# One shared set of PSUM banks for wide and narrow results, and ten loads issued by a second engine, in a scheduled attention and mixer kernel

## Chip, cores and metric

The kernel runs on one core of one Trainium2 chip. The metric is the device time of one execution in microseconds (us), less is better. A profiled execution also has a span, the time from its first to its last instruction, which is about 1.8 us shorter. Profiles are single executions: that of the kernel before took 214.4 us, 1.8 us less than its median, so a difference of two spans can be off by some us, and the medians decide. "Before" and "after" are the kernel without and with the change.

## The reference

Two parts run one after the other. The first is a recurrence over 768 steps for 4 batches and 8 heads of 40 numbers, from six inputs of 3.9 MB each. The second mixes its output over the tokens and the channels.

```python
for t in range(S):                                     # S = 768
    y[:, :, t] = einsum('bhd,bhde->bhe', rt, state)
    Sa = einsum('bhde,bhe->bhd', state, at)
    state = state * wt[:, :, None, :] - einsum('bhd,bhe->bhde', Sa, bt) + einsum('bhd,bhe->bhde', vt, kt)
# ... x = y with the heads side by side
theta = x @ w_theta
yr = einsum('ts,bsd->btd', w_tok_r, x * cos(theta))
yi = einsum('ts,bsd->btd', w_tok_i, x * sin(theta))
u = x + yr + yi
out = u + maximum(u @ w_ch, 0)
```

The kernel cuts the recurrence into 24 tiles of 128 tokens (6 in each batch). For each tile it loads w, a, k, b and v (r comes for two tiles at a time), makes decay products, transposes, four 128x1024 score products ("lamu", "lamv", "psi", "phi") with a masked eviction (a copy out of PSUM) each, and small products for the state. The mixer's rows ("row") need all of a batch, and the work of later tiles is laid over them.

## The kernel before

The kernel is written as a list of 1,457 operations. Each has an engine, an estimated cost, and the keys that it reads and writes. A list scheduler in the kernel lays the operations out in time by priority, assigns the banks of PSUM (the memory that takes TensorE's results, used here as eight banks), and emits the instructions in the order of the estimated starts. Nothing is reordered on the chip: in the traces each engine takes its instructions in this order, all 3,344 matmuls among them. The scheduler thus gives a planned length (208.2 us before). A framework beneath the kernel adds the semaphores.

```python
BANKS, DOUBLE = 8, 4
SP_DEPTH = 3600.0
# ...
def find(o):                                   # the scheduler looks for a free bank, or a pair
    n = o.new[1]
    if n == 2:
        c = [(max(bank_free[b], bank_free[b + 1]), (b, b + 1))
             for b in range(0, DOUBLE, 2)
             if not bank_held[b] and not bank_held[b + 1]]
        return min(c) if c else None
    c = [(bank_free[b], (b,)) for b in range(DOUBLE, BANKS) if not bank_held[b]]
    return min(c) if len(c) > o.spare else None
# ...
doubles = [psum.tile([128, 2, 512], FP32, name=f"ps_d{i}") for i in range(DOUBLE // 2)]
singles = [psum.tile([128, 512], FP32, name=f"ps_s{i}") for i in range(BANKS - DOUBLE)]
def ps(key):
    h = plan.home[key]
    return doubles[h[0] // 2] if len(h) == 2 else singles[h[0] - DOUBLE]
# ...
def loads(i):                                  # w, k, b, a, v of tile i, all from SyncE
    for key, dst, src in load(i):
        add("SP", "load", i, lambda dst=dst, src=src: nc.sync.dma_start(out=dst, in_=src),
            650, [], [key], work=1030)
# ...
for o in plan.order():                         # emission
    # ... (ScalarE's table loads)
    o.fn()
```

So four of the eight banks are two pairs, each one tile of two banks, for the scores. The other four are four tiles of one bank each, for transposes, rows and small products.

## Time and profile before

| | before |
|---|---|
| time, median (lowest to highest) | 216.2 us (215.5 to 216.7) |
| span of the profiled run | 212.6 us |
| length that the kernel's own scheduler planned | 208.2 us |
| TensorE: 3,344 matmuls, streaming need | 169.6 us |
| TensorE beyond streaming: changes of row mode / gaps over 60 ns / small ones | 20.1 / 11.4 / 3.8 us |
| changes between 64-row and 128-row matmuls | 130 |

The two TensorE lines need a word. The profile's busy time counts a matmul from start to end, but matmuls overlap. The Trainium skill, "Perfetto Trace Analysis", section "Identifying the Most-Contended Engine", says for this reason that matmul busy time is not a good measure of closeness to the limit, and this trace agrees: 195.1 us busy against 169.6 us of streaming. I therefore add the times from one matmul's start to the next one's. The least time in which one follows another of its kind is streaming (56 ns for 128 columns, 136 for 320). What goes beyond it at a change of row mode, in a gap over 60 ns, or in small steps, is the second line.

From the page of the kernel before: the span, TensorE's busy time, and the engines' shares of the chain that ended last.

```profile
span 212.6 us, 8107 instructions
...
PE 195.1 (92%) x3344; PEld 156.3 (74%) x3344; DVE 165.5 (78%) x252; ACT 148.6 (70%) x340; POOL 117.4 (55%) x173
...
PE 78%; DVE 7%; ACT 4%; issue 4%; DMA 3%; POOL 2%; SPq 1%; DVEq 0%; ACTq 0%; POOLq 0%
```

From the table of windows of the kernel before: for each stretch its length, then each engine's busy time with its instruction count, the granted TensorE clock, the DMA share and GB/s.

```profile
0.00:10.00 10.00, 3.84 (x39) 2.90 (x39) 6.33 (x48) 3.82 (x7) 3.39 (x14) 1.00 0.92 168
...
40.00:50.00 10.00, 8.94 (x194) 7.43 (x194) 8.53 (x9) 9.39 (x21) 8.43 (x13) 1.00 0.93 172
...
60.00:100.00 40.00, 38.72 (x716) 31.61 (x714) 33.40 (x43) 33.32 (x74) 30.71 (x45) 1.00 0.93 165
100.00:150.00 50.00, 49.93 (x911) 41.11 (x908) 43.85 (x56) 38.64 (x90) 30.43 (x43) 1.00 0.92 176
```

TensorE is short of work in the first 60 us (12.8 us idle, 6.2 of them in the first 10), where the DMA engines are full; after that it is hardly idle.

The rows of the mixer, in the groups of instructions by line, show how little TensorE waits (last field: its idle time just before these instructions):

```profile
L724 PE MATMUL ps_s<-zr,wtok_r 128*128 128x320 bf16 x144 | 40.7, 300 | 0.0
L724 PE MATMUL ps_s<-zi,wtok_i 128*128 128x320 bf16 x144 | 40.6, 299 | 0.0
```

And from the timeline (start, duration, instruction), a piece of one row, whose matmuls start every 130 to 140 ns:

```profile
151.11 0.30 PE L724 MATMUL ps_s<-zr,wtok_r 128*128 128x320 bf16 x1
...
151.24 0.30 PE L724 MATMUL ps_s<-zi,wtok_i 128*128 128x320 bf16 x1
...
151.38 0.30 PE L724 MATMUL ps_s<-zr,wtok_r 128*128 128x320 bf16 x1
```

### The profile page before, as it was taken

The page shows a single profiled execution, that of the slowest core. Times are in us where ns is not written, and L with a number is a line of the kernel's source. Part 1 is how long each engine was busy: PE and PEld are TensorE (multiplying, and loading weights), DVE is VectorE, ACT ScalarE, POOL GpSimd, SP SyncE. Part 2 cuts the span into 40 slices and gives each one's busy share as a digit, 9 for nine tenths or more (in the row PEclk, how much of TensorE's full clock was granted, in tenths as well). Part 3 has the DMA queues.
Part 4 walks back from the last instruction along what each step waited for, and adds up shares of the span by engine and source line. Part 5 has one row for each costly group of instructions (what it writes and reads, how often), then busy time and mean ns, then how long its engine had stood idle before and what let it go on. Part 6 is the DMA issues. An engine that isn't in the chain of part 4 may idle for free.

```text
span 212.6 us, 8107 instructions
## 1 busy us (share of the span) xinstructions
PE 195.1 (92%) x3344; PEld 156.3 (74%) x3344; DVE 165.5 (78%) x252; ACT 148.6 (70%) x340; POOL 117.4 (55%) x173
## 2 busy tenths in 40 slices
PE   1686899888998999999999999999999999999993
PEld 1464777776786777888878888887788887777771
DVE  7537796989889779869897889978979899744533
ACT  3375858799989969968787676599967996642101
POOL 5003358578765997857688315477667488050000
PEclk9999999999999999999999999999999999999999
DMA  7998989999799999975999899977997110011222
GB/s 118 221 191 170 178 166 175 177 181 185 148 162 194 162 166 193 190 123 111 244 161 197 163 180 178 183 133 172 183 201 145 35 34 3 0 34 71 84 96 93
DMA packets 134181, 30.82 MB, mean 145 GB/s; under 512 B 125824, under 2 KB 134144, under 8 KB 134144
## 3 DMA queue, kind: packets, MB, share of 16 engines
q1 hardware_dynamic: 131712, 27.54, 66.1%
q0 software_dynamic: 2432, 2.77, 8.8%
q8 instruction: 26, 0.43, 0.9%
q14 instruction: 11, 0.09, 0.1%
HBM read 29.13 MB, written 3.93 MB: 156 GB/s over the span
## 4 chain that ended last, share of the span: by engine, by line
PE 78%; DVE 7%; ACT 4%; issue 4%; DMA 3%; POOL 2%; SPq 1%; DVEq 0%; ACTq 0%; POOLq 0%
PE ps_s L724 19%; PE ps_s L398 13%; PE ps_d L522 11%; PE ps_s L670 9%; PE ps_s L625 4%; PE ps_s L573 3%; PE ps_s L505 3%; PE ps_s L591 2%; DVE phi L527 2%; PE ps_s L654 2%; DVE psi L527 2%; PE ps_s L772 2%; DMA raw_v<-in_v_dram 2%; PE ps_d L448 2%; PE ps_s L652 2%
## 5 line engine op out<-in xcount | busy, mean ns | idle before, releaser
L468 POOL TENSOR_TENSOR kb<-raw_kb,ex 128x320 bf16<-128x320 f32 x44 | 37.3, 863 | 32.4 <-ACT ex L460 30.9
L724 PE MATMUL ps_s<-zr,wtok_r 128*128 128x320 bf16 x144 | 40.7, 300 | 0.0
L724 PE MATMUL ps_s<-zi,wtok_i 128*128 128x320 bf16 x144 | 40.6, 299 | 0.0
L527 DVE TENSOR_TENSOR psi<-ps_d,mask_p 128x1024 bf16<-128x1024 f32 x24 | 29.3, 1220 | 7.4 <-PE ps_d L522 7.3
L527 DVE TENSOR_TENSOR lamu<-ps_d,mask_p 128x1024 bf16<-128x1024 f32 x24 | 29.3, 1220 | 4.7 <-PE ps_d L522 4.2
L527 DVE TENSOR_TENSOR lamv<-ps_d,mask_p 128x1024 bf16<-128x1024 f32 x24 | 29.1, 1218 | 3.0 <-PE ps_d L522 2.9
L527 DVE TENSOR_TENSOR phi<-ps_d,mask_n 128x1024 bf16<-128x1024 f32 x24 | 29.2, 1217 | 0.7 <-PE ps_d L522 0.6
L472 POOL TENSOR_TENSOR ah<-raw_a,ex 128x320 bf16<-128x320 f32 x22 | 19.0, 863 | 16.3 <-ACT ex L460 7.6
L706 POOL TENSOR_TENSOR zr<-cs,x 128x320 bf16<-128x320 f32 x23 | 17.8, 791 | 12.9 <-ACT cs L694 12.9
L460 ACT ACTIVATE ex<-ps_d 128x648 f32<-128x648 f32 x24 | 17.2, 716 | 7.7 <-PE ps_d L456 4.6
L734 DVE TENSOR_TENSOR u<-ps_s,x 128x320 bf16<-128x320 f32 x24 | 11.7, 489 | 11.2 <-PE ps_s L724 11.1
L401 ACT COPY uT<-ps_s 128x192 f32<-128x192 f32 x24 | 7.7, 320 | 17.1 <-PE ps_s L625 17.0
L706 POOL TENSOR_TENSOR zi<-cs,x 128x320 bf16<-128x320 f32 x23 | 17.7, 791 | 2.1 <-ACT cs L694 2.0
L522 PE MATMUL ps_d<-aT,kbT 64*128 64x128 bf16 x384 | 17.2, 222 | 1.1 <-ACT aT L401 0.5
L401 ACT COPY kbT<-ps_s 128x512 f32<-128x512 f32 x24 | 14.3, 595 | 4.6 <-PE ps_s L398 3.9
L724 PEld LDWEIGHTS <-wtok_r 128*128 128x128 bf16 x144 | 14.0, 97 | 4.5
L724 PEld LDWEIGHTS <-wtok_i 128*128 128x128 bf16 x144 | 14.0, 98 | 3.6
L398 PE MATMUL ps_s<-ident,kb 128*128 128x128 bf16 x192 | 15.4, 223 | 1.3 <-DVE kb L468 1.3
L743 DVE SCALAR_TENSOR_TENSOR oo<-ps_s,u 128x320 f32<-128x320 f32 x24 | 11.6, 486 | 5.2 <-PE ps_s L670 5.2
L522 PEld LDWEIGHTS <-kbT 64*128 64x128 bf16 x384 | 11.6, 96 | 5.2 <-issue 1.7
L654 PE MATMUL ps_s<-kb,lamu 128*128 128x40 bf16 x192 | 15.0, 180 | 0.5 <-DVE lamu L527 0.4
L652 PE MATMUL ps_s<-kb,lamv 128*128 128x40 bf16 x192 | 15.4, 180 | 0.0
(113 smaller groups left out, 556.3 us busy)
## 6 DMA issues: line engine op xcount, KB each, us to landing
raw_w<-in_w_dram SPq DMA_DIRECT2D x24, 160.0 KB, 3.8
raw_kb<-in_k_dram SPq DMA_DIRECT2D x24, 160.0 KB, 4.3
raw_kb<-in_b_dram SPq DMA_DIRECT2D x24, 160.0 KB, 4.2
raw_a<-in_a_dram SPq DMA_DIRECT2D x24, 160.0 KB, 4.1
raw_v<-in_v_dram SPq DMA_DIRECT2D x24, 160.0 KB, 3.9
raw_r<-in_r_dram SPq DMA_DIRECT2D x24, 160.0 KB, 3.5
out_dram<-oo SPq DMA_DIRECT2D x24, 160.0 KB, 2.3
wrow_r<-in_moe_w_tok_r_dram POOLq DMA_DIRECT2D x6, 192.0 KB, 4.7
```

The lines of the kernel that those rows point to most:

```text
L398: nc.tensor.transpose(out=dst[:, c:c + 128], in_=pair(src, g), identity=ident)
L401: nc.scalar.copy(out=out.bitcast(FP32), in_=in_)
L460: add("ACT", "exp", i, lambda: nc.scalar.activation(out=ex, in_=ps(pk).rearrange("p a b -> p (a b)")[:, 512 - DM:512 + DM + 8], func=AF.Ex ...
L468: lambda j=j: (nc.vector if fast else nc.gpsimd).tensor_tensor(out=paired(kb[:, j])[:, :, :, 0:D], in0=natural(raw_kb[s4][:, j]), in1=invW ...
L472: lambda: (nc.vector if fast else nc.gpsimd).tensor_tensor(out=paired(ah)[:, :, :, 0:D], in0=natural(raw_a[s4]), in1=Wi, op=ALU.mult),
L522: nc.tensor.matmul(t[:, q, g, :], lhsT=lhs[rows(q), g * 128:(g + 1) * 128], rhs=rhs[rows(q), g * 128:(g + 1) * 128], start=True, stop=True)
L527: add("DVE", kindm, i, lambda: nc.vector.tensor_tensor(out=dst.rearrange("p a b c -> p (a b) c"), in0=ps(p).rearrange("p a (g c) -> p (a g ...
L652: nc.tensor.matmul(o, lhsT=lamv[:, p, g, :], rhs=kb[:, 0, h, 0:D], start=first, stop=False, skip_group_check=True)
L654: nc.tensor.matmul(o, lhsT=lamu[:, p, g, :], rhs=kb[:, 1, h, 0:D], start=False, stop=True, skip_group_check=True)
L670: nc.tensor.matmul(dst, lhsT=lhs[:, kt, :], rhs=rhs[:, kt, :], start=kt == 0, stop=kt == 2)
L706: nc.vector if fast else nc.gpsimd).tensor_tensor(
L724: nc.tensor.matmul(ps(pk)[:, 0:DM], lhsT=wtok[nm][:, s, j * 128:(j + 1) * 128], rhs=zs[c][:, s], start=n == 0 and c == 0, stop=n == NT - 1 ...
```

## The change

The intent was threefold. All eight banks should serve both sizes of result, so that four scores or eight small results may be open at once. The v loads of the first ten tiles should be issued by ScalarE beside SyncE's loads, with six buffers for a and v. And the order of the same instructions was tuned anew for this.

```diff
-SP_DEPTH = 3600.0
+SP_DEPTH = 4600.0
+SECOND = dict(v=10)
...
-                     for b in range(0, DOUBLE, 2)
+                     for b in range(0, BANKS, 2)
...
-            c = [(bank_free[b], (b,)) for b in range(DOUBLE, BANKS) if not bank_held[b]]
+            c = [(bank_free[b], (b,)) for b in range(BANKS) if not bank_held[b]]
...
-    doubles = [psum.tile([128, 2, 512], FP32, name=f"ps_d{i}") for i in range(DOUBLE // 2)]
-    singles = [psum.tile([128, 512], FP32, name=f"ps_s{i}") for i in range(BANKS - DOUBLE)]
+    doubles = [psum.tile([128, 2, 512], FP32, name=f"ps_{i}") for i in range(BANKS // 2)]
...
     def ps(key):
         h = plan.home[key]
-        return doubles[h[0] // 2] if len(h) == 2 else singles[h[0] - DOUBLE]
+        d = doubles[h[0] // 2]
+        return d if len(h) == 2 else d[:, h[0] % 2, :]
...
+        last = None
         for key, dst, src in load(i):
-            add("SP", "load", i,
-                lambda dst=dst, src=src: nc.sync.dma_start(out=dst, in_=src),
-                650, [], [key], work=1030)
+            name = key[0][4:]
+            if i < SECOND.get(name, 0):
+                add("ACT", "l" + name, i,
+                    lambda dst=dst, src=src: nc.scalar.dma_start(out=dst, in_=src),
+                    430, [], [key], work=930, after=[last])
+            else:
+                last = add("SP", "l" + name, i,
+                    lambda dst=dst, src=src: nc.sync.dma_start(out=dst, in_=src),
+                    600, [], [key], work=930)
...
```

Cut from this: a and v in six buffers (`raw_a[i % 6]` for `raw_a[s4]`), new values of all priorities, a term for changes of row mode in the choice of the next operation, and a table of 1,452 single offsets of priorities. A load is now planned with 930 ns of DMA instead of 1,030.

## The prediction

> **What bounds it now.** Two things.
>
> Up to about 60 us, DMA. In the table of windows the DMA share is 0.90 to 1.08 in every 10 us up to 60, at 164 to 189 GB/s. The packet records say why: 122,880 of 134,194 packets are 160 bytes, median 14 ns, so 16 engines reach at most 183 GB/s. One tile (six 160 KB loads) takes 5.6 to 6 us to arrive, and TensorE lacks work: idle 12.8 of the first 60 us.
>
> Later, TensorE: busy 99.9 of the 100 us from 100 to 200, and 78% of the chain that ended last. Matmuls overlap, so I add start-to-start times. A 128-column matmul follows its like after 56 ns, 320 columns after 136, 40 columns after 25, a 64-row score matmul after 28 in the mean (26 taken). All 3,344 need 169.6 us. First to last start is 204.8 us, so 35 us is not streaming: 20.1 at the 130 changes between 64-row and 128-row matmuls, 11.4 in other gaps over 60 ns, 3.8 in small ones. A change in and out costs 87+122 = 209 ns by itself (112 instead of 25 ns going in, 148 instead of 26 coming out): 65 pairs are 13.6 us, the other 6.5 us is waiting there. The first 60 us hold 46 of the changes and 18.4 of those 31.5 us.
>
> **What the change does.**
> 1. All eight PSUM banks serve both sizes: four double results open instead of two, or eight singles instead of four. Three or four score groups can run in a row, and a slow DVE mask (1.22 us each, 96 of them) blocks the next group less.
> 2. Ten early v loads go to ScalarE's queue; a and v get six buffers, not four. The Trainium skill, "DMA: Bandwidth & Descriptors", section "Issuing engines are not separate DMA queues", says both queues run on the same 16 engines and only issue time is saved. The trace shows them full, so I expect at most part of the 0 to 8% that the share leaves. SyncE loses ten issues (median 0.69 us); ScalarE gains them, by my estimate at 0.5 to 0.8 us, 5 to 8 us of the first 60, where it is 38 to 94% busy: mostly idle time.
> 3. A retuned order of the same instructions; the 169.6 us of matmul stays.
>
> **On the critical path.** Changes from 130 to about 100: 15 pairs, -3 us. Waits at changes and gaps (17.9 us) down by a quarter: -4. Earlier data: -2. ScalarE issues: +0.5. Sum -8.5 us.
>
> Predicted **207.5 us**, 8 times in 10 within **202 to 213**. Chances: faster by over 2% **0.80**, within 2% **0.17**, slower **0.03**.
>
> **What would show it.** Streaming need near 170 us; under 115 changes; TensorE idle in the first 60 us below 11; DMA rate to 60 us up no more than 5%; last v load issued before 158 us (now 159.8); ScalarE issues under 1 us each; still about 45 us of TensorE work after the last load.
>
> **What would make it wrong.** Two queues may really move more (then 200 us is possible), or ScalarE may stall for microseconds in an issue[...]. Shared banks may leave no aligned pair free, so scores wait. The order was laid out for estimated durations; where engines or loads run late, in-order engines pass every error on, and the gain shrinks.

## The result

| | before | after |
|---|---|---|
| time, median (lowest to highest) | 216.22 us (215.53 to 216.68) | 255.12 us (254.44 to 256.89) |
| ratio of the times | | 1.1815 (95%: 1.1743 to 1.1887) |
| span of the profiled run | 212.6 us | 255.1 us |
| planned length | 208.2 us | 205.1 us |
| changes of row mode: number, us | 130, 20.1 | 110, 23.4 |
| gaps over 60 ns, small ones | 11.4, 3.8 us | 48.7, 5.6 us |
| start of the last instructions behind plan | 4.3 us | 49.9 us |

All ratios here are the mean time of one kernel's fast runs over that of the other's of the same rounds, so they are not quite the ratio of the medians quoted. The one recorded for e8, 1.0097, cannot come from its fast runs alone, since their highest, 216.86 us, over the lowest of the kernel before, 214.83 us, is 1.0094: it has the slow run in it. The means of the fast runs alone give 1.003.

The change is slower by 18%; its plan had promised 3 us less. The kernel before runs 4.3 us behind its plan at the end. After runs 9.1 us behind at 40 us, 16.8 at 75, 26.3 at 130 and 49.9 at the end. So the loss isn't one accident, it accumulates all along.

The page after:

```profile
span 255.1 us, 8022 instructions
...
PE 209.3 (82%) x3344; PEld 163.5 (64%) x3344; DVE 169.0 (66%) x252; ACT 151.8 (60%) x340; POOL 118.0 (46%) x173
...
PE 51%; ACT 23%; DVE 8%; issue 6%; DMA 4%; SPq 3%; POOL 3%; ACTq 0%; DVEq 0%; POOLq 0%
```

The work is the same 3,344 matmuls, but ScalarE now has 23% of the chain of waits (4% before), although its own busy time hardly rose (148.6 to 151.8 us). Something makes TensorE wait for ScalarE and ScalarE for TensorE.

The same windows after:

```profile
0.00:10.00 10.00, 2.56 (x19) 1.69 (x19) 5.38 (x47) 2.84 (x4) 3.39 (x14) 1.00 0.91 163
...
40.00:50.00 10.00, 8.14 (x181) 6.83 (x178) 6.76 (x7) 7.03 (x18) 5.47 (x9) 1.00 0.66 118
...
60.00:100.00 40.00, 32.16 (x542) 25.23 (x540) 26.65 (x34) 24.34 (x56) 26.96 (x40) 0.96 0.76 134
100.00:150.00 50.00, 43.62 (x744) 34.67 (x742) 35.85 (x45) 36.11 (x77) 29.93 (x43) 1.00 0.86 163
```

Between 100 and 150 us TensorE starts 744 matmuls instead of 911, and every other engine is less busy as well. The DMA share has fallen too. No engine and no queue is full, which speaks for waits between the engines.

The rows after, first as groups, then what ended TensorE's idle time before them (us, times):

```profile
L938 PE MATMUL ps<-zr,wtok_r 128*128 128x320 bf16 x144 | 41.1, 299 | 7.2 <-ACT rT L723 1.9
...
L938 PE MATMUL ps<-zi,wtok_i 128*128 128x320 bf16 x144 | 41.1, 299 | 0.0
```

```profile
its engine sat idle before it (us, times) until:
  issue: 9.8, 17
  ACT rT L723: 1.9, 4
  ACT uT L608: 0.9, 2
  DVE oo L957: 0.8, 2
  ACT aT L608: 0.7, 2
  ACT kbT L608: 0.7, 1
```

The first line, "issue", is idle time of the weight loads of this line of the kernel; the others are of the matmuls. A row multiplies zr by wtok_r. It reads neither rT nor kbT nor aT, and its bank isn't theirs. Yet it waits for their evictions. One such place in the timeline after (the brackets give the idle time before and what ended it):

```profile
146.30 0.30 PE L938 MATMUL ps<-zi,wtok_i 128*128 128x320 bf16 x1
...
146.64 0.59 ACT L608 COPY kbT<-ps 128x512 f32<-128x512 f32 x1
...
147.28 0.30 PE L938 MATMUL ps<-zr,wtok_r 128*128 128x320 bf16 x1 [0.67 <-ACT kbT L608]
...
147.41 0.30 PE L938 MATMUL ps<-zi,wtok_i 128*128 128x320 bf16 x1
```

The eviction of kbT ends at 146.64 + 0.59 = 147.23 us; the next matmul of the row starts 50 ns later. In the scheduler's plan the row is in bank 3 and kbT in bank 2, the two halves of one tile. Before, TensorE was never idle before a matmul of a row (0.0 us).

The reason that suggests itself lies in `ps()`. Before, two small results in two banks were two tiles. After, they are two halves of one tile. The framework keeps its order by tile, so a matmul into one half may have to wait for an eviction of the other half. To see how much of the loss this touches, I set each operation's measured start against everything that the scheduler says it needs (its inputs, its bank, the instruction before it on its engine). I count it as late when it starts over 150 ns after all of these. A start within 100 ns after the end of another engine's access of the other bank of the same tile is counted in the last columns.

| | late operations | on TensorE | on ScalarE | on VectorE | of these next to the other half | time of these (PE, ACT, DVE) |
|---|---|---|---|---|---|---|
| before | 10 | 7 (1.2 us) | 3 on ScalarE and VectorE together | | 0 | 0 |
| after | 176 | 76 (30.9 us) | 61 (28.2 us) | 39 (17.8 us) | 150 | 27.1, 25.6, 14.2 us |

This is a count of coincidences, so it needed experiments.

### The profile page after: what moved, and what is told of

It is laid out like the page before. It is cut to its first block, busy times and chain, and to the rows that moved or that the text cites. A ratio compares the mean times of both kernels' runs of the same rounds, so it can differ in the third digit from the quotient of the medians.

```text
span 255.1 us, 8022 instructions
## 1 busy us (share of the span) xinstructions
PE 209.3 (82%) x3344; PEld 163.5 (64%) x3344; DVE 169.0 (66%) x252; ACT 151.8 (60%) x340; POOL 118.0 (46%) x173
## 4 chain that ended last, share of the span: by engine, by line
PE 51%; ACT 23%; DVE 8%; issue 6%; DMA 4%; SPq 3%; POOL 3%; ACTq 0%; DVEq 0%; POOLq 0%
PE ps L938 14%; PE ps L605 8%; PE ps L884 7%; PE ps L736 5%; ACT rT L723 3%; SPq L631 3%; PE ps L839 3%; DMA raw_kb<-in_b_dram 2%; PE ps L719 2%; DVE x L875 2%; DMA raw_r<-in_r_dram 2%; ACT ex L674 2%; ACT kbT L608 2%; ACT nx L781 2%; ACT th L894 2%
## 5 line engine op out<-in xcount | busy, mean ns | idle before, releaser
L938 PE MATMUL ps<-zr,wtok_r 128*128 128x320 bf16 x144 | 41.1, 299 | 7.2 <-ACT rT L723 1.9
L938 PE MATMUL ps<-zi,wtok_i 128*128 128x320 bf16 x144 | 41.1, 299 | 0.0
L741 DVE TENSOR_TENSOR psi<-ps,mask_p 128x1024 bf16<-128x1024 f32 x24 | 29.2, 1218 | 10.1 <-PE ps L736 9.6
L741 DVE TENSOR_TENSOR lamu<-ps,mask_p 128x1024 bf16<-128x1024 f32 x24 | 29.2, 1216 | 3.7 <-PE ps L736 3.1
L741 DVE TENSOR_TENSOR lamv<-ps,mask_p 128x1024 bf16<-128x1024 f32 x24 | 28.9, 1216 | 1.2 <-PE ps L736 1.1
L741 DVE TENSOR_TENSOR phi<-ps,mask_n 128x1024 bf16<-128x1024 f32 x24 | 29.1, 1215 | 0.7 <-PE ps L736 0.4
L920 POOL TENSOR_TENSOR zr<-cs,x 128x320 bf16<-128x320 f32 x23 | 17.8, 792 | 16.4 <-ACT cs L908 13.1
L608 ACT COPY kbT<-ps 128x512 f32<-128x512 f32 x24 | 14.2, 592 | 11.8 <-PE ps L605 6.4
L674 ACT ACTIVATE ex<-ps 128x648 f32<-128x648 f32 x24 | 17.0, 717 | 5.8 <-PE ps L670 3.9
L605 PE MATMUL ps<-ident,kb 128*128 128x128 bf16 x192 | 16.6, 234 | 4.1 <-DVE kb L682 1.9
L736 PE MATMUL ps<-aT,kbT 64*128 64x128 bf16 x384 | 17.2, 225 | 2.6 <-ACT kbT L608 2.0
```

The costliest lines, as they stand in the source:

```text
L605: nc.tensor.transpose(out=dst[:, c:c + 128], in_=pair(src, g), identity=ident)
L608: nc.scalar.copy(out=out.bitcast(FP32), in_=in_)
L674: add("ACT", "exp", i, lambda: nc.scalar.activation(out=ex, in_=ps(pk).rearrange("p a b -> p (a b)")[:, 512 - DM:512 + DM + 8], func=AF.Ex ...
L736: nc.tensor.matmul(t[:, q, g, :], lhsT=lhs[rows(q), g * 128:(g + 1) * 128], rhs=rhs[rows(q), g * 128:(g + 1) * 128], start=True, stop=True)
L741: add("DVE", kindm, i, lambda: nc.vector.tensor_tensor(out=dst.rearrange("p a b c -> p (a b) c"), in0=ps(p).rearrange("p a (g c) -> p (a g ...
L920: nc.vector if fast else nc.gpsimd).tensor_tensor(
```

## The experiments

The expectations name the theories by letters. F: false waits between the halves of a two-bank tile make the loss. Its rivals in the first runs are Q, the second queue (issues of loads hold up ScalarE), and O, the new order, which may not suit the chip. Three came up after the first runs. Q2: ScalarE stands still in its issues of loads, since these wait for earlier loads. D: the planned times of loads are too hopeful, whoever issues them. E: issues of loads hold up any busy engine. That a and v have six buffers was not tried alone on the changed kernel. Wherever an experiment alters PSUM, the order of engines on each single bank was checked in the built program: in after and e1 all 7,723 pairs of accesses of one bank by different engines stay ordered (7,614 in the kernel before).

| run | what it is | median us | before, same chip | ratio (95%) | planned us | behind plan at the end |
|---|---|---|---|---|---|---|
| before | | 216.2 | | | 208.2 | 4.3 |
| after | the change | 255.1 | 216.2 | 1.1815 (1.1743 to 1.1887) | 205.1 | 49.9 |
| e1_waits_off | after, without waits between halves | 220.30 | 215.79 | 1.0199 (1.0162 to 1.0237) | 205.1 | 13.7 |
| e2_halves_before | before, small results as halves | 263.11 | 215.79 | 1.2177 (1.2130 to 1.2223) | 208.2 | 51.6 |
| e4_one_queue | after, all loads from SyncE | 268.74 | 215.79 | 1.2450 (1.2410 to 1.2490) | 217.6 | 49.4 |
| e5_sync_issue | e1, the ten v issues on SyncE | 216.26 | 215.41 | 1.0040 (0.9991 to 1.0089) | 205.1 | 9.2 |
| e6_queue_only | before, the ten v issues on ScalarE | 222.54 | 215.41 | 1.0319 (1.0274 to 1.0365) | 208.2 | 12.5 |
| e7_split_banks | after, banks divided as before | 237.36 | 215.41 | 1.1011 (1.0956 to 1.1066) | 219.3 | 16.1 |
| e8_pool_issue | e1, the ten v issues on GpSimd | 216.65 (216.44 without its slow run) | 215.16 | 1.0097 (1.0029 to 1.0165), with its slow run | 205.1 | 7.7 |
| e9_split_sync | e7, the ten v issues on SyncE | 231.45 | 215.16 | 1.0731 (1.0659 to 1.0803) | 219.3 | 11.1 |

All eight gave correct results. The granted clock of these kernels was a little below that of the kernel before (after 0.98, e1 0.98 to 0.99, e7 0.96 to 0.97, before 1.00). It explains little: the runs of e1 at 0.977 and at 0.992 have spans of 218.9 and 218.1 us, and the run of e5 at 1.000 is no shorter (214.6 us) than that at 0.988 (213.9 us).

### e1_waits_off: the same kernel without waits between halves

```diff
+        have = nc.n_instructions()
         o.fn()
+        o.insts = list(itertools.islice(nc.all_instructions(), have, None))
+        at = {b for k in set(o.reads) | set(o.writes) if k[0] == "ps" for b in plan.home[k]}
+        if len(at) == 1:                          # works in one bank only
+            b, = at
+            keep = [x for q in o.pre for x in q.insts]
+            for x in o.insts:
+                for e in {"PE", "ACT", "DVE"} - {o.eng}:
+                    tc.declare_no_dep(x, group=f"{e}{b ^ 1}", keep=keep,
+                                      reason="the other bank of the pair")
+                tc.add_to_no_dep_group(f"{o.eng}{b}", x)
```

Order, banks, queues and work are those of after. Only the framework is told that accesses of two different banks don't depend on each other, and true dependencies are kept.

> The changed kernel with the same instruction order, the same banks and the same two load queues; only the semaphore waits that order one bank of a two-bank tile behind the other bank are declared unnecessary (the built program was searched: all 7,723 pairs of accesses to one bank by two engines stay ordered). Theory F (false waits between the halves of a shared tile are the loss): near the 205 us that the kernel's own schedule plans plus the 4 us by which the kernel before missed its own, so 207 to 214 us, PE gaps over 60 ns fall from 48.7 to under 16 us. Theory O (the retuned order does not suit the chip): 245 to 256 us. Theory Q (load issues on ScalarE stall it and everything behind it): 245 to 256 us.

Measured: 220.30 us, span 218.9. So 36.2 of the 42.5 us of added span are gone, by this declaration alone; by the medians it is 34.8 of 38.9 us. The interval of its ratio (1.0162 to 1.0237) leaves open whether it is still 2% slower than the kernel before. The rows wait no more (7.2 us to 0.2):

```profile
L939 PE MATMUL ps<-zr,wtok_r 128*128 128x320 bf16 x144 | 41.5, 303 | 0.2 <-DVE phi L742 0.2
L939 PE MATMUL ps<-zi,wtok_i 128*128 128x320 bf16 x144 | 41.4, 302 | 0.0
```

Late operations fell from 176 to 15, and none of the 15 starts next to the other half. F is borne out as the main cause. But the time lies 6 us above the range that F gave, and gaps fell only to 20.3 us where below 16 was expected. Something else costs time, and e1 shows where: the lag behind plan jumps from 6.4 to 11.8 us between 60 and 75 us. ScalarE's timeline just there:

```profile
58.34 0.37 ACT L609 COPY nuT<-ps 128x256 f32<-128x256 f32 x1
61.75 0.37 ACTq L628 DMA_DIRECT2D raw_v<-in_v_dram  x1
62.17 1.00 ACT L909 ACTIVATE cs<-th 128x960 f32<-128x960 f32 x1 [3.46 <-DMA raw_v<-in_v_dram]
```

Its next instruction is the issue of a v load, which stands till 61.75 us. The order planned it for 52.3. In the built program the framework hands eight completion semaphores to the loads in turn, over both queues, so an issue waits until the load eight places earlier has landed. Here that one is the v load of tile 11, issued by SyncE at 56.73 us and landed at about 61.7. On ScalarE, which takes its instructions in order, all evictions stand behind this wait. There were five such waits at v issues in e1: 0.67, 1.57, 1.33, 0.80 and 3.04 us. That is theory Q2.

### e2_halves_before: the kernel before, its small results declared as halves

```diff
-    singles = [psum.tile([128, 512], FP32, name=f"ps_s{i}") for i in range(BANKS - DOUBLE)]
+    halves = [psum.tile([128, 2, 512], FP32, name=f"ps_h{i}") for i in range((BANKS - DOUBLE) // 2)]
...
-        return doubles[h[0] // 2] if len(h) == 2 else singles[h[0] - DOUBLE]
+        if len(h) == 2:
+            return doubles[h[0] // 2]
+        return halves[(h[0] - DOUBLE) // 2][:, h[0] % 2, :]
```

The order, the banks and the queue are those of before. Only the declaration differs.

> The kernel before, its order, banks, queue and buffers untouched; only its four single-bank tiles are declared as the halves of two two-bank tiles, which adds the waits between halves and nothing else. Theory F: clearly slower, 228 to 255 us (half of the banks are affected, against all in the change). Theories O and Q: 216 us, within 1%.

Measured: 263.11 us, more than was expected and more than the whole change costs. Of 220 late operations 189 start next to the other half. The rows wait as they do in after, also for evictions that they don't need:

```profile
L726 PE MATMUL ps_h<-zr,wtok_r 128*128 128x320 bf16 x144 | 40.9, 298 | 9.7 <-ACT rT L511 1.7
```

So another declaration of the same four banks, with nothing else changed, cost the old kernel 47 us. Why it is more than expected is argued and not tested: four banks carry all the small results, so a half may nearly always have a busy neighbour. Together, e1 and e2 show the cause in both directions.

### e4_one_queue: the change with all loads from SyncE

```diff
-SECOND = dict(v=10)
+SECOND = dict()
```

> The changed kernel with all loads back on SyncE's queue; shared tiles stay. The schedule plans 218 us for it instead of 205. Theory F: still far above its plan, 250 to 270 us. Theory Q: the stall goes, 218 to 225 us. Theory O: 255 to 270 us.

Measured: 268.74 us, in the range that F gave, and in that of O, which this run doesn't tell from F. The second queue is not what made the change slow: without it the loss is larger, as the plan of this order is longer without it (217.6 us), and the lag at the end is the same (49.4 us after 49.9). Of 180 late operations 148 start next to the other half.

### e6_queue_only: the kernel before with the ten v loads issued by ScalarE

```diff
-    raw_v = sb("raw_v", [128, H, D], FP32, 4)
+    raw_v = sb("raw_v", [128, H, D], FP32, 6)
...
-                lambda dst=dst, src=src: nc.sync.dma_start(out=dst, in_=src),
+                lambda dst=dst, src=src, key=key: (
+                    nc.scalar if key[0] == "raw_v" and i < 10 else nc.sync).dma_start(out=dst, in_=src),
```

The places of the issues in the planned order are kept. The skill's rule in the expectation is the one that the prediction quotes from "DMA: Bandwidth & Descriptors", section "Issuing engines are not separate DMA queues".

> The kernel before with its tiles, banks and order untouched; only the ten early v loads are issued by ScalarE at the places of the schedule (v has six buffers so that no issue waits for a buffer). Theory Q2: slower, 218 to 228 us, with waits of over 1 us at issues on ScalarE. Rival D and the skill's rule that only issue time is saved: 214 to 218 us.

Measured: 222.54 us, so the second queue (with six buffers for v) costs the old kernel 3.2%. One wait is the largest:

```profile
43.09 0.48 ACT L442 ACTIVATE lw<-raw_w 128x320 bf16<-128x320 f32 x1
47.81 0.38 ACTq L418 DMA_DIRECT2D raw_v<-in_v_dram  x1
48.23 0.44 ACT L578 ACTIVATE nu<-ps_s 128x320 bf16<-128x320 f32 x1 [4.65 <-DMA raw_kb<-in_b_dram]
```

For 4.65 us ScalarE evicts nothing while its issue waits until a load of b has landed. TensorE is stopped by it. The window of this experiment:

```profile
40.00:50.00 10.00, 4.81 (x96) 4.06 (x93) 4.12 (x5) 3.92 (x11) 3.28 (x5) 0.91 1.03 186
```

Against 8.94 us of TensorE's busy time in the same window before, it is 4.81. The DMA engines meanwhile are as full as ever. At 60 us this kernel is 10.1 us behind its plan, the kernel before 2.2.

### e5_sync_issue and e8_pool_issue: without false waits, the v loads issued elsewhere

```diff
 # e5, against e1                              (e8: nc.gpsimd in its place)
-                    lambda dst=dst, src=src: nc.scalar.dma_start(out=dst, in_=src),
+                    lambda dst=dst, src=src: nc.sync.dma_start(out=dst, in_=src),
```

The planned order of TensorE, VectorE and GpSimd, and of all evictions, stays that of e1; only the engine that issues the ten loads differs.

> The run with the waits off, but the ten early v loads are issued by SyncE at the places that the schedule gives them; the order of instructions on TensorE, VectorE and GpSimd is identical, ScalarE's too except for the ten issues that are gone. Theory Q2 (in the run with the waits off, a load issue on ScalarE waits until the load eight places before it has landed, because eight completion semaphores are handed round both queues, and holds up ScalarE's evictions; three such waits of 1.4, 0.8 and 3.1 us lie on its chain): 208 to 215 us, and the lag behind the schedule at 75 us falls from 11.8 to under 7 us. Rival D (the schedule's estimates of loads are too hopeful, whoever issues them): 218 to 222 us, lag unchanged.

> As the run with the waits off, the ten early v loads now issued by GpSimd, another in-order engine, at the places of the schedule; its loads use completion semaphores of their own (the built program shows other names), of which no other load in flight holds one. Theory Q2 (the shared semaphores make the wait, not the issue on a busy engine): no wait over 0.5 us at GpSimd's v issues, lag at 75 us under 7 us, 213 to 218 us. Rival E (any busy in-order engine is held up by load issues): waits again, 219 to 224 us.

Measured: 216.26 us (e5, about a microsecond outside the range given) and 216.65 us (e8, inside; 216.44 without its slow run). At 75 us, e5 is 3.5 us and e8 5.8 us behind plan, e1 11.8. From e1 to e5 the ratio to the kernel before falls from 1.0199 to 1.0040, which is 1.6% of 215.4, or 3.4 us; the spans fall by 4.5 us. The two runs are of different chips, so I take it as about 4 us. That is the price of ScalarE's waiting issues in the new order. In e8 no wait over 0.2 us stands at GpSimd's issues, though each takes it 0.93 us:

```profile
L628 POOL DMA_DIRECT2D raw_v<-in_v_dram x10: 902/928/963, 5.6 to 62.4; - x10
```

Behind ScalarE's issues stand evictions; behind SyncE's there are only other loads and the stores of the output. It isn't quite free there either: in e5 SyncE issues the b and k loads of tile 10 at 69.2 and 69.9 us, where the plan had 63.8 and 64.7; in e8 it is 64.2 and 65.4.

### e3_split_banks, e7_split_banks and e9_split_sync: the new order with banks divided as before

```diff
-                     for b in range(0, BANKS, 2)
+                     for b in range(0, DOUBLE, 2)
...
-            c = [(bank_free[b], (b,)) for b in range(BANKS) if not bank_held[b]]
+            c = [(bank_free[b], (b,)) for b in range(DOUBLE, BANKS) if not bank_held[b]]
...
 # the two kinds of tiles, and ps(), as in the kernel before; a row may leave one bank less spare:
-                new=(pk, 1) if n == 0 else None, spare=(2 if bi < B - 1 else 1),
+                new=(pk, 1) if n == 0 else None, spare=(1 if bi < B - 1 else 0),
 # e9 besides: the ten v issues on SyncE
```

> The changed kernel with the division of banks of before (two double tiles, four single tiles, none shared), the planner told so and the reserve of single banks for row sums lowered by one so that it finds an order; ScalarE queue, six buffers and all priorities of the change stay. Its schedule plans 219 us, because the priorities were tuned for eight free banks. Theory F: 219 to 226 us, close to its plan. Theories O and Q: 245 us or more.

e3 didn't build: the file held another setting of the spare banks of a row, with which the scheduler found no bank. It was mended as e7.

> The changed kernel with the division of banks of before (two double tiles, four single tiles, nothing shared; the reserve of single banks for row sums lowered by one so that an order is found); ScalarE queue, six buffers and all priorities of the change stay. Its own schedule plans 219 us. Theory F: no lag from false waits, 221 to 233 us with up to 10 us for the ScalarE issues. Theory O (priorities that do not suit the chip): 245 us or more.

> The changed kernel with the banks divided as before and, besides, the ten v loads issued by SyncE at the same places. Schedule 219 us. In the run with divided banks the waits at ScalarE's issues add up to 8.6 us. Theory Q2: 226 to 232 us, against 237 with ScalarE's queue. Rival (something else in the order makes the lag): 235 to 239 us.

Measured: 237.36 us (e7, 4 us above its range) and 231.45 us (e9, in its range). The false waits are gone here too, since small results have their own tiles, and e7 lies well below after even though its plan is 14 us longer. The miss of e7 is ScalarE again: six waits at its v issues sum to 8.6 us, and e9, which has none, is faster by the 5.9 us between the medians. Set e9 (plan 219.3) against e5 (plan 205.1): 14.2 us in plan, and 1.0731 - 1.0040 = 6.9% or 15 us measured. So the measured times follow the plans. That the shared banks are worth these 15 us is not shown, since an order tuned as finely as this loses about as much by any change to the planner: with 929 ns instead of 930 planned for a load, and the eight banks shared, its own plan is 217.9 us. The old priorities did as well with divided banks.

## Why the prediction was wrong

It gave 207.5 us (202 to 213), and 0.03 for slower. Measured: 255.1.

**What held.** The streaming need stayed 169.6 us. Changes of row mode fell to 110 (under 115 was said), and without the false waits they cost less: 15.9 us in e1 and 15.7 in e5 against 20.1, where the prediction took off 3 us. Two queues gave little more bandwidth. In the first 60 us after moves 164 GB/s, the kernel before 173. With the same order e1 moves 177 and e8 182 against 174 in e5, where SyncE alone issues; e7 171 against 175 in e9; and e6 184 against 173 in the kernel before. So it is between 2% less and 6% more. The Trainium skill, "DMA: Bandwidth & Descriptors", section "Issuing engines are not separate DMA queues", says that only issue time is saved; these traces agree within those few per cent, and no run tells whether the 5 and 6% of e8 and e6 come from the second queue. A ScalarE issue itself is short: 375 ns in the median, less than the estimate of 0.5 to 0.8 us.

**The step that failed** is "Waits at changes and gaps (17.9 us) down by a quarter: -4". The time at changes and in gaps went from 31.5 to 72.1 us (23.4 + 48.7). With 209 ns taken off for each pair of changes, as the prediction did, its 17.9 us of waits became about 60.6. Even without the false waits they didn't fall: they are about 24.7 us in e1 and 21.3 in e5. I took a bank only as room that may be free or held, so shared room could only take waits away. But `d[:, h[0] % 2, :]` is also a statement to the framework about what depends on what. As halves of one tile, two independent results wait for each other. This costs about 35 us here (after to e1, by the medians) and 47 us in the kernel before (before to e2). The diff showed that line, and the list of what could go wrong didn't name it. TensorE's idle time in the first 60 us was to fall below 11 us; it rose from 12.8 to 15.8. In e1 and e5 it is 12.6 and 12.1, so the 2 us of "Earlier data" didn't come either.

**A second step was mis-sized:** "ScalarE issues: +0.5". It measured about 4 us from e1 to e5, and 6.9 us (3.2% of 215.4) in e6. The prediction named a stall of microseconds in an issue as a risk. What was seen is a wait for a completion semaphore shared by both queues. In after itself it hardly shows: only one of its v issues waited over 1 us (1.02 us), perhaps since that kernel ran behind its loads anyway. The last v load was issued at 174.2 us, where the prediction said before 158.

**And the gain wasn't there.** Even with both costs taken away, e5 comes to 216.3 us and e8 to 216.4 (its fast runs) against 215.4 and 215.2 before. So 207.5 would have been wrong without any false wait. The plan itself had only 3.1 us of gain (208.2 to 205.1), less than the 8.5 that I summed, and the chip doesn't give these: e5 ends 9.2 us behind its plan, the kernel before 4.3. About 4 of these 9.2 us arise between 75 and 100 us (3.5 to 7.6). There the b and k loads of tile 10 land at 75.4 and 77.0 us, where the plan had 69.9 and 70.8, with the DMA engines full (share 0.98 to 1.05). As said, SyncE issued these two over 5 us late; in e8 they land at 70.3 and 70.9, as planned, and yet e8 loses 3.4 us between 60 and 75 us.

The planned time of a load says more. The plan of after gives 160 KB 930 ns, the plan of before 1,030, and by the packets' mean of 14.9 to 15.1 ns (1,024 packets on 16 engines) a load takes 954 to 969 at best. I set 960 in both, kept each order and its banks as they are, and let the scheduler's own rules lay out the times again. After is then planned at 208.0 us, before at 207.7. So the 3.1 us of planned gain is nearly all the more hopeful 930. This is a calculation, not a run. (To let the scheduler choose anew with 960 gives 221.7 us, but that shows only that the order is disturbed: with 929, a shorter load, it gives 217.9.) What remains open is the split of the last 5 us of lag between e5 and before, in single profiles that differ by some us, and whether a better order exists.

## What to carry to other kernels

A slice of a tile isn't a tile: when several independent results share one declared buffer, look in the built program or the trace for instructions that start some tens of ns (on TensorE here 51 to 54) after an access of a neighbouring slice that they don't need, and give each result its own tile or declare the independence. Put a load's issue only on an engine for which it is no harm to wait, or make sure that the load whose semaphore it takes over has landed. And weigh a retuned order by what its own plan gains when the order is kept and the durations are set to those measured: here 30 ns more for each load took 2.9 of the 3.1 us.

## What the Trainium skill lacked or had wrong

- "PSUM — Partial Sum Buffer", section "PSUM bank collisions raise a hardware error", asks to guard PSUM by bank and quadrant. This case agrees: e1 drops the waits between the two banks of a tile and stays correct, at 220.3 us instead of 255.1. The page lacks the other side of the rule. A two-bank tile in the framework is guarded as a whole, which cost about 35 us here and 47 us in e2. No page that I found has it.
- "DMA: Bandwidth & Descriptors", section "Issuing engines are not separate DMA queues", says that issuing from several engines saves only the sequencer's time. The rate of the first 60 us was between 2% lower and 6% higher with the second queue (e7 171 against 175 GB/s, e6 184 against 173), so that holds within a few per cent. It lacks the cost: an issue on ScalarE stood up to 3 us (e1) and over 4 us (e6) behind an earlier load, and all evictions with it, so the old kernel became 3.2% slower.
- The same page, section "Why a DMA increments its semaphore by 16 and not by 1", asks for one semaphore per in-flight slot. Eight shared over two queues, as here, keep to that only by making the ninth issue wait for the first. The page doesn't say on which engine such a wait is cheap: with the v issues on SyncE the time was 1.004 of that before (e5), on ScalarE 1.020 (e1). GpSimd's loads have semaphores of their own, and no wait over 0.2 us was seen there (e8).
- No page that I found says how long a wait between two engines through PSUM takes to pass on: TensorE's late starts next to the other half came 51 to 52 ns (the middle 80%) after the end of ScalarE's access and 53 to 54 ns after VectorE's.
